# Three x tiles transposed on TensorE, the fourth by DMA transpose, its plain load moved behind

## The chip, the cores and the metric

One core of one Trainium2 chip. The metric is the device time of one execution in microseconds (us), as the median of several executions. The kernel computes a gated mix of a linear-attention block and a token-mixing MLP for one sequence of 2048 tokens and 512 features, in bf16.

## The reference, cut to what matters

```python
x = A_x                                     # [1, 2048, 512]
g = _sigmoid((x * gate_w).sum(-1, keepdims=True))
a = _A_ref(x, A_wqkv, A_wo)                 # q, k, v = x @ wqkv; 32 heads of 16; linear attention; @ wo
b = _B_ref(x, B_w1, B_b1, B_w2, B_b2)       # layernorm; tokens mixed by w1, gelu, w2
return g * a + (1 - g) * b
```

The change touches only the opening of the kernel: the first step is `k = x @ wk` for 16 tiles of 128 tokens. A matmul on TensorE contracts over the partitions, so it needs x transposed (features on partitions). The kernel gets some of the transposed tiles by transposing on TensorE (PE) and the others by a DMA transpose straight from DRAM.

## The kernel before

The parts that matter. PE is TensorE, DVE is VectorE, ACT is ScalarE and SP is SyncE; the results of the matmuls stand in PSUM until DVE or ACT copies them out. The PSUM tiles are named in the profiles: `kacc` for the k matmuls, `gacc` for the products of x with phi(k) (phi is the positive map that the linear attention applies to k), `uacc` for the first matmuls of the token-mixing MLP. `xs` holds x with tokens on partitions, `xT` holds it transposed, `wk_sb` is the k part of the weight in four chunks of 128 rows. The first x tiles and the wk chunks are loaded on two queues (SP is `nc.sync`, ACT is `nc.scalar`):

```python
    load_x(nc.sync, 0, 1)
    load_x(nc.scalar, 1, 1)
    load_wk(nc.sync, 0)
    load_x(nc.scalar, 2, 1)
    load_x(nc.sync, 3, 1)
    for k, q in ((1, nc.scalar), (2, nc.sync), (3, nc.scalar)):
        load_wk(q, k)
    load_xT(4, 2)                 # DMA transpose of tiles 4 and 5
    load_xT(6, 2)
    load_x(nc.sync, 4, 4)
    for t0, n in ((8, 4), (12, 4)):
        load_xT(t0, n)
        load_x(nc.sync, t0, n)
    # ... wq, w1, wv, wo follow on the same queue
```

PE starts with six warm-up matmuls on constants. Then four x tiles are transposed on PE and copied out of PSUM (`transpose_tile`), and the k matmuls of the first tiles run chunk by chunk, as the chunks arrive:

```python
    HEADS = 4
    transpose_tile(0, False)      # False: copied out by DVE, True: by ACT
    transpose_tile(1, True)
    transpose_tile(2, False)
    ln_step(0)
    for k in range(2):
        for t in range(HEADS - 1):
            k_part(t, (k,))
    transpose_tile(HEADS - 1, True)
    ln_step(1)
    for t in range(HEADS):
        k_part(t, range(2 if t < HEADS - 1 else 0, ND))
        k_phi(t)
    LAG = 4
    # ...
    for t in range(HEADS, NT):
        k_part(t, range(ND))
        k_phi(t)
        g_tile(t - LAG)           # the gacc matmuls: x tile (t - 4) with phi(k)
        # ... statistics of the layernorm on DVE
```

Of the kernel before, what the change touches and what calls it, by code (L numbers as in the profile page):

```python
# [8 lines left out]
ALU = mybir.AluOpType  # L9
AX = mybir.AxisListType  # L10
# [5 lines left out]
def kernel(  # L16
# [13 lines left out]
    nc = tc.nc  # L30
    P = nc.NUM_PARTITIONS
# [9 lines left out]
    ND = D // P  # L41
# [25 lines left out]
    def keep(shape, dtype, name):  # L67
        return persist.tile(shape, dtype, name=name, tag=name)

    def bank(name, dtype=FP32):  # L70
        return ps.tile([P, SC], dtype, name=name, tag="bank")

    xs = keep([P, NT, D], BF16, "xs")
    hs = keep([P, NT, D], BF16, "hs")
    xT = keep([P, ND, S], BF16, "xT")
# [9 lines left out]
    Z32 = keep([P, ND * 40], BF16, "Z32")  # L85
# [7 lines left out]
    ident = keep([P, P], BF16, "ident")  # L93
    maskH = keep([P, 8], BF16, "maskH")
    maskQ = keep([P, 2], BF16, "maskQ")
    gw_b = keep([P, D], BF16, "gw_b")
    brow = keep([P, P], BF16, "brow")
# [10 lines left out]
    mhalf = keep([P, TPC], FP32, "mhalf")  # L108
    ones_f = keep([P, 1], FP32, "ones_f")
    warm = nc.const_aps.tensor(1.0, (P, SC), BF16)  # L110

    def mm(o, lhsT, rhs, start, stop, **kw):
        nc.tensor.matmul(o, lhsT=lhsT, rhs=rhs, start=start, stop=stop, **kw)  # L113

    def block_mask(m, cols, width):
        nc.gpsimd.memset(m, 1.0)
        nc.gpsimd.affine_select(
            out=m, in_=m, compare_op=ALU.is_ge, fill=0.0, base=0,
            pattern=[[-HEAD, cols], [0, width]], channel_multiplier=1,
        )  # L120
        nc.gpsimd.affine_select(
            out=m, in_=m, compare_op=ALU.is_ge, fill=0.0, base=HEAD - 1,
            pattern=[[HEAD, cols], [0, width]], channel_multiplier=-1,
        )
# [3 lines left out]
    def load_x(q, t0, n):  # L128
        q.dma_start(out=xs[:, t0 : t0 + n, :], in_=x_view[:, t0 : t0 + n, :])

    def load_wk(q, k):
        q.dma_start(out=wk_sb[:, k, :], in_=wqkv_view[:, k, D : 2 * D])

    def load_xT(t0, n):
        nc.sync.dma_start(
            out=xT[:, :, t0 * P : (t0 + n) * P], in_=X[t0 * P : (t0 + n) * P, :], transpose=True
        )
# [2 lines left out]
    load_x(nc.scalar, 1, 1)  # L140
    load_wk(nc.sync, 0)
    load_x(nc.scalar, 2, 1)
    load_x(nc.sync, 3, 1)
    for k, q in ((1, nc.scalar), (2, nc.sync), (3, nc.scalar)):
        load_wk(q, k)
    load_xT(4, 2)
    load_xT(6, 2)
    load_x(nc.sync, 4, 4)
    for t0, n in ((8, 4), (12, 4)):
        load_xT(t0, n)  # L150
# [3 lines left out]
    for c, (j0, nb) in enumerate(w1_chunks):  # L154
        w = wpool.tile([P, NT, FB * P], BF16, name="w1c", tag="wc")
        w1c.append(w)
        for t0 in range(0, NT, 8) if c == 0 else (0,):
            t1 = t0 + 8 if c == 0 else NT
            nc.sync.dma_start(
                out=w[:, t0:t1, : nb * P], in_=w1_view[:, t0:t1, j0 * P : (j0 + nb) * P]  # L160
# [2 lines left out]
            nc.sync.dma_start(out=wv_sb[:], in_=wqkv_view[:, :, 2 * D : 3 * D])  # L163
            nc.sync.dma_start(out=wo_sb[:], in_=wo_view)

    nc.vector.memset(ones_f[:], 1.0)
    nc.vector.memset(mhalf[:], -0.5)
    nc.vector.memset(Z32[:], 0.0)
    nc.gpsimd.memset(ident[:], 0.0)
    nc.gpsimd.affine_select(  # L170
        out=ident[:], in_=ident[:], compare_op=ALU.not_equal, fill=1.0, base=0,
        pattern=[[-1, P]], channel_multiplier=1,
    )
    block_mask(maskH[:].rearrange("p (a b) -> p a b", b=1), 8, 1)

    nc.vector.tensor_reduce(
        out=maskQ[:], in_=maskH[:].rearrange("p (a m) -> p m a", m=2), op=ALU.max, axis=AX.X
    )
    nc.gpsimd.memset(brow[:], 0.0)

    def load_small():
        nc.gpsimd.dma_start(out=brow[0:NF, :], in_=B_b1.rearrange("(f q) -> f q", q=P))
        nc.gpsimd.dma_start(out=brow[NF : NF + NT, :], in_=B_b2.rearrange("(f q) -> f q", q=P))
        nc.gpsimd.dma_start(
            out=gw_b[:], in_=gate_w.rearrange("(o d) -> o d", o=1).to_broadcast([P, D])
        )
# [11 lines left out]
    def transpose_tile(t, on_act):  # L198
        pt = bank("pt", BF16)
        for k in range(ND):  # L200
            nc.tensor.transpose(pt[:, k * P : (k + 1) * P], xs[:, t, k * P : (k + 1) * P], ident[:])  # L201
        dst = xT[:, :, t * P : (t + 1) * P]
        src = pt[:].rearrange("p (k s) -> p k s", k=ND)
        if on_act:
            nc.scalar.activation(out=dst, in_=src, func=ACT.Copy)  # L205
        else:
            nc.vector.tensor_copy(out=dst, in_=src)
# [13 lines left out]
    def k_part(t, ks):  # L221
        if t not in kaccs:
            kaccs[t] = bank("kacc")
        for k in ks:
            mm(
                kaccs[t][:], xT[:, k, t * P : (t + 1) * P], wk_sb[:, k, :],
                k == 0, k == ND - 1,
            )

    def k_phi(t):  # L230
        phi(pk[:, t, :], kaccs.pop(t))
# [11 lines left out]
    def ln_shift(g):  # L243
        s = slice(g * TPC, (g + 1) * TPC)
        nc.vector.scalar_tensor_tensor(  # L245
            out=nmr[:, s], in0=mv[:, s, 0], scalar=-1.0, in1=rstd[:, s],
            op0=ALU.mult, op1=ALU.mult,
        )

    def ln_apply(t):  # L250
        nc.scalar.activation(  # L251
            out=hs[:, t, :], in_=xs[:, t, :], func=ACT.Identity,
            scale=rstd[:, t : t + 1], bias=nmr[:, t : t + 1],
        )
# [3 lines left out]
    def g_tile(t):  # L258
        if not gacc:
            gacc.extend(bank("gacc") for _ in range(ND))  # L260
        for k in range(ND):
            mm(gacc[k][:], xs[:, t, k * P : (k + 1) * P], pk[:, t, :], t == 0, t == NT - 1)
# [15 lines left out]
    def ln_step(u):  # L278
        ln_stats(u)
        if u % TPC == TPC - 1:  # L280
            ln_rstd(u // TPC)

    HEADS = 4
    transpose_tile(0, False)
    transpose_tile(1, True)
    transpose_tile(2, False)
    ln_step(0)
    for k in range(2):
        for t in range(HEADS - 1):
            k_part(t, (k,))  # L290
    transpose_tile(HEADS - 1, True)
    ln_step(1)
    for t in range(HEADS):
        k_part(t, range(2 if t < HEADS - 1 else 0, ND))
        k_phi(t)
    LAG = 4
    LN_LAG = 3
    APPLY = 9
    for t in range(HEADS, NT):
        k_part(t, range(ND))  # L300
        k_phi(t)
        g_tile(t - LAG)
        if t > LAG:
            ln_step(t - LN_LAG)
        if t == TPC - 1 + LN_LAG:
            load_small()
        if t >= APPLY:
            ln_apply(t - APPLY)
        if t % TPC == 0 and t >= 2 * TPC:
            ln_shift(t // TPC - 2)  # L310
# [143 lines left out]
    for j in range(NB0, NF):  # L454
        c, jj = divmod(j, FB)
# [18 lines left out]
        out=gg[:], in0=gth[:], scalar1=0.5, scalar2=0.5, op0=ALU.mult, op1=ALU.add  # L474
    )
    nc.vector.tensor_scalar(
        out=c1[:], in0=gth[:], scalar1=-0.5, scalar2=0.5, op0=ALU.mult, op1=ALU.add
# [3 lines left out]
    for t in range(NT):  # L481
        c, tl = divmod(t, TPC)
        aps = bank("aps")
        for j in range(ND):
# [3 lines left out]
            out=a_sc[:], in_=aps[:], func=ACT.Identity,  # L488
            scale=gg[:, t : t + 1], bias=c2[:, t : t + 1],
        )  # L490
        for c0, W in ((0, D - P), (D - P, P)) if t == NT - 1 else ((0, D),):
            cs = slice(c0, c0 + W)
            yps = bank("yps")
            for f in range(NF):
# [6 lines left out]
                out=ot[:, :W], in0=yps[:, :W], scalar=c1[:, t : t + 1], in1=a_sc[:, cs],  # L501
# [35 lines left out]
```

## Time and profile before

| | before |
|---|---|
| device time, median of 3 (lowest to highest) | 164.56 us (164.44 to 164.77) |
| span of the profiled execution | 162.5 us |
| PE busy | 158.1 us (97%) |
| DVE busy / ACT busy | 89.5 / 63.3 us |

The profile page of the kernel before, the lines for the whole span and for the chain that ended last:

```profile
span 162.5 us, 2183 instructions
...
PE 158.1 (97%) x823; PEld 72.8 (45%) x837; DVE 89.5 (55%) x210; ACT 63.3 (39%) x97; POOL 17.5 (11%) x34
...
## 4 chain that ended last, share of the span: by engine, by line
PE 97%; issue 0%; DVE 0%
```

The chain is PE from end to end. So work that leaves PE's stream is a gain, and work that moves between the other engines is not, unless PE comes to wait for it.

The timeline of PE in the opening of the kernel before (start, duration, engine, line, operation, output<-inputs, shapes, count):

```profile
2.93 0.63 PE L113 MATMUL wps<-const-bfloat16-1.0 128*128 128x512 bf16 x1
3.55 1.47 PE L201 MATMUL pt<-ident,xs 128*128 128x128 bf16 x12
4.82 1.97 PE L113 MATMUL kacc<-wk_sb,xT 128*128 128x512 bf16 x6
6.62 0.39 PE L201 MATMUL pt<-ident,xs 128*128 128x128 bf16 x4
6.84 3.19 PE L113 MATMUL kacc<-wk_sb,xT 128*128 128x512 bf16 x14
9.86 0.59 PE L113 MATMUL gacc<-pk,xs 128*128 128x512 bf16 x2
```

The reader should see the order: twelve transposes of tiles 0 to 2, six k matmuls (wk chunks 0 and 1 of three tiles), then four transposes of tile 3 between 6.62 and 6.84, then fourteen k matmuls, and the first gacc matmul at 9.86. The durations of neighbouring lines overlap because matmuls are pipelined; the useful number is the distance of two starts. The first matmul on chunk 1 waited about 0.1 us (its start at 5.97 is 0.34 us after the one before it).

The timeline of SP's DMA queue in the kernel before, without the first line and those after 3.70 (the duration is the time to issue, not to land):

```profile
1.27 0.41 SPq L132 DMA_DIRECT2D wk_sb<-in_A_wqkv_dram  x1
1.73 0.42 SPq L129 DMA_DIRECT2D xs<-in_A_x_dram  x1
2.20 0.43 SPq L132 DMA_DIRECT2D wk_sb<-in_A_wqkv_dram  x1
3.70 2.74 SPq L135 DMA_TRANSPOSE xT<-in_A_x_dram  x2
```

The DMA view of the kernel before, restricted to the moment 1.74 us (wk chunk 1, on ACT's queue) and to 3.70 us (the first DMA transpose); the last column is the time from issue to landing:

```profile
wk_sb<-in_A_wqkv_dram ACTq DMA_DIRECT2D x1, 128.0 KB, 4.2
...
xT<-in_A_x_dram SPq DMA_TRANSPOSE x1, 4.0
```

So chunk 1 landed at about 5.9 (5.93 in the trace) and its first matmul started at 5.97; the first DMA transpose (tiles 4 and 5) landed at 7.66, and was wanted at 8.78.

### The profile page before, as it was taken

To read this page: it belongs to the slowest core of one execution; us is meant where nothing else is said; L and a number is where in the kernel's file an instruction comes from. 1 tells how busy PE (TensorE), PEld (TensorE's weight loads), DVE (VectorE), ACT (ScalarE), POOL (GpSimd) and SP (SyncE) were. 2 spreads that over 40 slices of the span, in tenths; PEclk is the share of its full clock that TensorE was granted. 3 is DMA by queue.
4 is the path that set the end of the run, shared out by engine and by line. 5 is a ranking of instruction groups with operands and counts; after the bars stand their busy time and mean duration, and the time that the engine had idled before them with its cause. 6 is when DMAs were issued, how large, how long until landed. Compare 5 with 4: busy or idle time off the path is not lost.

```text
span 162.5 us, 2183 instructions
## 1 busy us (share of the span) xinstructions
PE 158.1 (97%) x823; PEld 72.8 (45%) x837; DVE 89.5 (55%) x210; ACT 63.3 (39%) x97; POOL 17.5 (11%) x34
## 2 busy tenths in 40 slices
PE   7999999999999999999999999999999999999993
PEld 3544444444444444444444444444444444444452
DVE  0599999967999999519995301166211111111112
ACT  3463386648667483212865113111122222111110
POOL 3000711200110000001415500050000000000000
PEclk9999999999999999999999999999999999999999
DMA  5999999999900006600892699822000001110001
GB/s 152 239 212 237 280 316 334 379 386 387 338 12 0 0 0 221 230 4 0 280 318 80 197 325 297 315 99 102 32 32 32 32 32 41 48 44 33 32 32 32
DMA packets 30057, 25.05 MB, mean 154 GB/s; under 512 B 7968, under 2 KB 29472, under 8 KB 30048
## 3 DMA queue, kind: packets, MB, share of 16 engines
q1 hardware_dynamic: 27744, 21.76, 43.4%
q0 software_dynamic: 1440, 2.38, 5.8%
q10 hardware_dynamic: 864, 0.79, 1.4%
q8 instruction: 6, 0.10, 0.3%
q14 instruction: 3, 0.02, 0.0%
HBM read 21.11 MB, written 2.23 MB: 144 GB/s over the span
## 4 chain that ended last, share of the span: by engine, by line
PE 97%; issue 0%; DVE 0%
PE uacc L113 30%; PE yps L113 30%; PE kacc L113 9%; PE aps L113 8%; PE gacc L113 8%; PE qacc L113 8%; PE wps L113 2%; PE pt L201 1%; PE denps L113 1%; PE kvps L113 0%; PE w2ps L113 0%; DVE ot L500 0%; PE pt L330 0%
## 5 line engine op out<-in xcount | busy, mean ns | idle before, releaser
L113 PE MATMUL uacc<-hs,w1c 128*128 128x512 bf16 x219 | 51.0, 379 | 0.4
L113 PE MATMUL yps<-uT,w2c 128*128 128x512 bf16 (+2 forms) x234 | 50.6, 366 | 0.2
L500 DVE SCALAR_TENSOR_TENSOR ot<-yps,c,a_sc 128x512 bf16<-128x512 f32 (+2 forms) x17 | 12.2, 720 | 45.2 <-PE yps L113 42.0
L113 PEld LDWEIGHTS <-w2c 128*128 128x128 bf16 x238 | 22.8, 98 | 25.9
L113 PEld LDWEIGHTS <-w1c 128*128 128x128 bf16 x224 | 21.8, 98 | 26.3 <-issue 0.2
L487 ACT ACTIVATE a_sc<-aps,c,gg 128x512 f32<-128x512 f32 x16 | 12.4, 777 | 46.7 <-PE aps L113 39.6
L324 ACT ACTIVATE uT<-uacc,bcol 128x512 bf16<-128x512 f32 x14 | 9.3, 688 | 21.7 <-PE uacc L113 21.7
L113 PE MATMUL aps<-W2sb,pqT 128*128 128x512 bf16 x63 | 16.2, 379 | 0.1
L113 PE MATMUL kacc<-wk_sb,xT 128*128 128x512 bf16 x63 | 16.2, 385 | 0.0
L113 PE MATMUL qacc<-xT,wq_sb 128*128 128x512 bf16 x63 | 16.2, 379 | 0.0
L113 PE MATMUL gacc<-pk,xs 128*128 128x512 bf16 x62 | 15.5, 379 | 0.1
L251 ACT ACTIVATE hs<-xs,nmr,rstd 128x512 bf16<-128x512 bf16 x16 | 12.8, 805 | 1.9 <-DVE nmr L245 1.9
L211 ACT ACTIVATE e<-qacc 128x512 bf16<-128x512 f32 x16 | 9.6, 597 | 9.2 <-PE qacc L113 8.3
L211 ACT ACTIVATE e<-kacc 128x512 bf16<-128x512 f32 x16 | 9.3, 595 | 6.9 <-PE kacc L113 5.6
L439 POOL DMA_DIRECT2D rex<-rd_dram x16 | 9.5, 602 | 22.9 <-DVE pqT L441 20.5
L215 DVE SCALAR_TENSOR_TENSOR pk<-kacc,e 128x512 bf16<-128x512 f32 x16 | 11.1, 692 | 0.6
L215 DVE SCALAR_TENSOR_TENSOR pqT<-qacc,e 128x512 bf16<-128x512 f32 x16 | 11.1, 692 | 0.6
L235 DVE BATCH_NORM_STATS2 stats<-xs 128x6 f32<-128x512 bf16 x16 | 10.9, 682 | 0.0
L212 DVE TENSOR_SCALAR e<-e 128x512 bf16<-128x512 bf16 x32 | 9.0, 281 | 3.3 <-ACT e L211 3.3
L426 DVE CUSTOM_DVE_ANT_0 junk<-xs,gw_b 128x512 bf16<-128x512 bf16 x16 | 9.8, 683 | 0.0
L276 DVE TENSOR_TENSOR zacc<-zacc,pk 128x512 f32<-128x512 f32 x14 | 9.6, 685 | 0.2
L113 PEld LDWEIGHTS <-xT 128*128 128x128 bf16 x64 | 6.3, 99 | 7.5 <-ACT xT L205 0.4
(61 smaller groups left out, 71.6 us busy)
## 6 DMA issues: line engine op xcount, KB each, us to landing
w2c<-in_B_w_dram SPq DMA_DIRECT2D x8, 896.0 KB, 6.2
w1c<-in_B_w_dram SPq DMA_DIRECT2D x2, 2048.0 KB, 14.0
w1c<-in_B_w_dram SPq DMA_DIRECT2D x3, 1024.0 KB, 11.6
rex<-rd_dram POOLq DMA_DIRECT2D x16, 128.0 KB, 3.5
out_dram<-ot SPq DMA_DIRECT2D x13, 128.0 KB, 1.7
xs<-in_A_x_dram SPq DMA_DIRECT2D x3, 512.0 KB, 5.2
wq_sb<-in_A_wqkv_dram SPq DMA_DIRECT2D x1, 512.0 KB, 6.1
wv_sb<-in_A_wqkv_dram SPq DMA_DIRECT2D x1, 512.0 KB, 10.6
```

Source lines behind the costliest of these rows:

```text
L113: nc.tensor.matmul(o, lhsT=lhsT, rhs=rhs, start=start, stop=stop, **kw)
L211: nc.scalar.activation(out=e[:], in_=acc[:], func=ACT.Exp)
L212: nc.vector.tensor_scalar(out=e[:], in0=e[:], scalar1=1.0, scalar2=PHI_EPS, op0=ALU.min, op1=ALU.add)
L215: nc.vector.scalar_tensor_tensor(out=dst, in0=acc[:], scalar=0.0, in1=e[:], op0=ALU.max, op1=ALU.add)
L235: nc.vector.bn_stats(out=stats[:], in_=xs[:, t, :])
L251: nc.scalar.activation(out=hs[:, t, :], in_=xs[:, t, :], func=ACT.Identity, scale=rstd[:, t : t + 1], bias=nmr[:, t : t + 1],)
L276: nc.vector.tensor_tensor(out=zacc[:], in0=first, in1=pk[:, t, :], op=ALU.add)
L324: nc.scalar.activation(out=uT[:, j, :], in_=acc[:], func=ACT.Gelu_apprx_tanh, bias=bcol[:, j : j + 1])
L426: nc.vector.tensor_tensor_reduce(out=junk[:], in0=xs[:, t, :], in1=gw_b[:], scale=1.0, scalar=0.0, op0=ALU.mult, op1=ALU.add, accum_out=gp ...
L439: nc.gpsimd.dma_start(out=rex[:], in_=src.unsqueeze(1).to_broadcast([8, HEAD, SC]))
L487: nc.scalar.activation(out=a_sc[:], in_=aps[:], func=ACT.Identity, scale=gg[:, t : t + 1], bias=c2[:, t : t + 1],)
L500: nc.vector.scalar_tensor_tensor(out=ot[:, :W], in0=yps[:, :W], scalar=c1[:, t : t + 1], in1=a_sc[:, cs], op0=ALU.mult, op1=ALU.add,)
```

## The change

Intent: PE no longer transposes tile 3. It comes by DMA transpose together with tile 4. The plain load of tile 3 (needed later, for the gacc matmul and the layernorm) moves behind the DMA transposes. A DVE copy that reads x tile 0 and writes into the destination of the first DMA transpose makes that transpose wait until tile 0 has landed (the copied values are overwritten). The memsets on DVE and GpSimd move up only so that this copy comes after them.

```diff
     load_x(nc.scalar, 2, 1)
-    load_x(nc.sync, 3, 1)
     for k, q in ((1, nc.scalar), (2, nc.sync), (3, nc.scalar)):
         load_wk(q, k)
-    load_xT(4, 2)
-    load_xT(6, 2)
+    # ... the memsets and masks, moved up unchanged
+    nc.vector.tensor_copy(
+        out=xT[:, :, 3 * P : 3 * P + 2],
+        in_=xs[:, 0, 0 : 2 * ND].rearrange("p (k c) -> p k c", k=ND),
+    )
+    load_xT(3, 2)
+    load_xT(5, 3)
+    load_x(nc.sync, 3, 1)
     load_x(nc.sync, 4, 4)
 # ... cut
-    HEADS = 4
+    HEADS = 3
 # ... cut
     for k in range(2):
-        for t in range(HEADS - 1):
+        for t in range(HEADS):
             k_part(t, (k,))
-    transpose_tile(HEADS - 1, True)
     ln_step(1)
     for t in range(HEADS):
-        k_part(t, range(2 if t < HEADS - 1 else 0, ND))
+        k_part(t, range(2, ND))
         k_phi(t)
 # ... cut
-        g_tile(t - LAG)
+        if t >= LAG:
+            g_tile(t - LAG)
```

More of the change, by code (lines that the diff above doesn't have):

```diff
@@ L142 @@
     load_x(nc.scalar, 2, 1)
-    load_x(nc.sync, 3, 1)
     for k, q in ((1, nc.scalar), (2, nc.sync), (3, nc.scalar)):
         load_wk(q, k)
-    load_xT(4, 2)
-    load_xT(6, 2)
+    nc.vector.memset(ones_f[:], 1.0)
+    nc.vector.memset(mhalf[:], -0.5)
+    nc.vector.memset(Z32[:], 0.0)
+    nc.gpsimd.memset(ident[:], 0.0)
+    nc.gpsimd.affine_select(
+        out=ident[:], in_=ident[:], compare_op=ALU.not_equal, fill=1.0, base=0,
+        pattern=[[-1, P]], channel_multiplier=1,
+    )
+    block_mask(maskH[:].rearrange("p (a b) -> p a b", b=1), 8, 1)
+    nc.vector.tensor_reduce(
+        out=maskQ[:], in_=maskH[:].rearrange("p (a m) -> p m a", m=2), op=ALU.max, axis=AX.X
+    )
+    nc.gpsimd.memset(brow[:], 0.0)
+    nc.vector.tensor_copy(
+        out=xT[:, :, 3 * P : 3 * P + 2],
+        in_=xs[:, 0, 0 : 2 * ND].rearrange("p (k c) -> p k c", k=ND),
+    )
+    load_xT(3, 2)
+    load_xT(5, 3)
+    load_x(nc.sync, 3, 1)
     load_x(nc.sync, 4, 4)
@@ L164 @@
             nc.sync.dma_start(out=wo_sb[:], in_=wo_view)
-    nc.vector.memset(ones_f[:], 1.0)
-    nc.vector.memset(mhalf[:], -0.5)
-    nc.vector.memset(Z32[:], 0.0)
-    nc.gpsimd.memset(ident[:], 0.0)
-    nc.gpsimd.affine_select(
-        out=ident[:], in_=ident[:], compare_op=ALU.not_equal, fill=1.0, base=0,
-        pattern=[[-1, P]], channel_multiplier=1,
-    )
-    block_mask(maskH[:].rearrange("p (a b) -> p a b", b=1), 8, 1)
-    nc.vector.tensor_reduce(
-        out=maskQ[:], in_=maskH[:].rearrange("p (a m) -> p m a", m=2), op=ALU.max, axis=AX.X
-    )
-    nc.gpsimd.memset(brow[:], 0.0)
     def load_small():
```

## The prediction

> **What bounds the kernel now.** TensorE. The page shows PE busy for 158.1 of 162.5 us at the full granted clock; the chain of waits is 97% PE. From 6.8 us on, matmuls follow each other at a 0.216 us pitch to the end. What leaves that chain is saved; moved DVE, ACT or DMA work saves nothing.
>
> **The opening (timeline, DMA landings).** x tiles 0, 1, 2 land at 3.50, 3.68, 4.37; wk chunk 0 at 4.16; x tile 3 at 5.71; wk chunks 1, 2, 3 at 5.93, 6.45, 6.62. PE waits for tile 0 (until 3.55), for the copies of tiles 1 and 2 out of PSUM (5.27, 5.54), and for wk chunk 1 (5.97). Then four transposes of tile 3 (6.62 to 6.84), six matmuls, tile 3's four from 8.14, tile 4's from 9.00. The first DMA transpose (tiles 4, 5) issues at 3.70, after x tile 1 landed (its semaphore slot makes it wait), and lands at 7.66; the second (6, 7) at 8.80.
>
> **What the change does.**
> 1. Removes four PE transposes of 0.055 us from the chain: -0.22 us. Certain.
> 2. Removes one ACT copy (0.60 us): off the chain.
> 3. Takes x tile 3 (128 KB) out of the early loads. wk chunk 2 moves into its place and should land near 5.7. Chunk 1, on which PE waits, is third on the ACT queue and competes with the third SP load as before: about 5.9 again, gain 0, perhaps 0.1 to 0.2.
> 4. The hold is a DVE copy of 128x8 (about 0.1 us, from the small DVE operations) after x tile 0. The transpose then issues near 3.7, as before: the old slot wait did the same by accident.
> 5. Tiles 3 and 4 by DMA transpose: same start, no x tile 3 ahead, landing 7.2 to 7.7. PE now wants it at 7.70 (6.62 + six matmuls, less the weight load). This is the tight spot: 0 to 0.5 us of margin, where before it had 1.1. A stall would eat the 0.22.
> 6. Tiles 5 to 7: landing about 9.4 (8.80 plus half of the 1.14 between the old two), wanted at 10.3. Later SP loads slip by about 1 us: x tile 3 by 12 (wanted 14.8), tiles 8 to 11 at 14.3 to 14.7 (was 13.52; wanted 15.5), w1 near 27.6 (wanted 33). No wait.
> 7. DVE is nearly full from 8 to 32 us; pk of the last tile is done at 31.85, its matmul runs at 32.31. DVE starts from the first exp, which also comes 0.22 sooner, so this margin stays.
>
> The Trainium skill ("DMA: Bandwidth & Descriptors", "Issuing engines are not separate DMA queues") says that transfers of different issuers share the same 16 DMA engines and interleave; in the trace wk chunks 1 to 3, from two issuers, land within 0.7 us. So taking out a load need not bring the awaited one sooner.
>
> **Prediction.** 164.56 - 0.22, a little less for wk, a little more for a possible stall: 164.35 us, 8 in 10 between 164.0 and 164.8. Faster by over 2%: 0.005; within 2%: 0.985; slower: 0.01.
>
> **What would show it.** 12 transposes on PE instead of 16; first gacc matmul near 9.65 (was 9.86), first uacc near 32.95 (was 33.17); no PE wait for the transposed tile; PE gap-free after 7 us.
>
> **What would make it wrong.** Tiles 3 and 4 landing after 7.7 (each 0.1 late costs 0.1), or their packets slowing wk chunks 1 and 3; chunk 1 landing much sooner (more gain); tiles 8 to 11 later than 15.5.

## The result, and the profile after

| | before | after |
|---|---|---|
| device time, median of 6 (lowest to highest) | 164.50 us (164.10 to 164.77) | 164.14 us (164.02 to 164.64) |
| ratio, 95% interval | | 0.9984 (0.9966 to 1.0002) |
| span of the profiled execution | 162.5 us | 162.5 us |
| PE busy | 158.1 us | 157.5 us |

A ratio here and below is the mean time of one kernel's fast runs over that of the other's fast runs of the same rounds, so it is not quite the ratio of the medians.

The time is inside the predicted range, 0.21 us below the predicted 164.35. The range also holds the time of the kernel before, so the time alone would not tell a right mechanism from a wrong one. But the two profiles have equal spans. The profiled executions took 164.22 (before, a quick one for that kernel) and 164.19 us (after, an ordinary one). A single pair of profiles therefore doesn't show where the gain is; it has to be taken apart.

The page of the kernel after, the lines that answer to those shown of before:

```profile
span 162.5 us, 2175 instructions
...
PE 157.5 (97%) x819; PEld 72.5 (45%) x833; DVE 89.4 (55%) x211; ACT 62.8 (39%) x96; POOL 17.5 (11%) x34
...
## 4 chain that ended last, share of the span: by engine, by line
PE 94%; DMA 3%; issue 1%; ACTq 1%; DVE 0%
```

The timeline of PE in the opening of the kernel after:

```profile
2.93 0.63 PE L113 MATMUL wps<-const-bfloat16-1.0 128*128 128x512 bf16 x1
3.47 1.32 PE L206 MATMUL pt<-ident,xs 128*128 128x128 bf16 x12
4.62 0.38 PE L113 MATMUL kacc<-wk_sb,xT 128*128 128x512 bf16 x1
5.19 0.61 PE L113 MATMUL kacc<-wk_sb,xT 128*128 128x512 bf16 x2 [0.19 <-ACT xT L210]
6.16 3.83 PE L113 MATMUL kacc<-wk_sb,xT 128*128 128x512 bf16 x17 [0.36 <-DMA wk_sb<-in_A_wqkv_dram]
9.82 0.59 PE L113 MATMUL gacc<-pk,xs 128*128 128x512 bf16 x2
```

The four transposes at 6.62 are gone, and seventeen k matmuls run without a break from chunk 1 to the first gacc matmul. In front of them is now a visible wait for wk chunk 1. "DMA 3%" in the page's chain is the flight of that load (4.4 us), at the end of which the wait ends. It is not new: before, chunk 1 was also the last thing PE waited for, but the wait was short enough to hide under the modelled end of the matmul ahead of it.

The timeline of SP's DMA queue in the kernel after, without the first line and those after 7.05:

```profile
1.27 0.89 SPq L132 DMA_DIRECT2D wk_sb<-in_A_wqkv_dram  x2
3.64 3.36 SPq L135 DMA_TRANSPOSE xT<-in_A_x_dram  x2
7.05 1.06 SPq L129 DMA_DIRECT2D xs<-in_A_x_dram  x2
```

The DMA view of the kernel after, restricted to 1.74 us (wk chunk 1, on ACT's queue) and to 3.64 us (the first DMA transpose):

```profile
wk_sb<-in_A_wqkv_dram ACTq DMA_DIRECT2D x1, 128.0 KB, 4.4
...
xT<-in_A_x_dram SPq DMA_TRANSPOSE x1, 4.1
```

The first DMA transpose issues where it did before (3.64 against 3.70) and lands at 7.72. Its first weight load on PE started at 7.88, so the margin was 0.16 us. Chunk 1 landed at 6.12, which is 0.19 us later than in the profile of before, and this ate the 0.22 us that the transposes had cost. The open question was whether that lateness belongs to the change or to the execution.

### The profile page after: what moved, and what is told of

Its sections match the earlier page's. It is cut to its first block, busy times and chain, and to the rows that moved or that the text cites. A ratio compares the mean times of both kernels' runs of the same rounds, so it can differ in the third digit from the quotient of the medians.

```text
span 162.5 us, 2175 instructions
## 1 busy us (share of the span) xinstructions
PE 157.5 (97%) x819; PEld 72.5 (45%) x833; DVE 89.4 (55%) x211; ACT 62.8 (39%) x96; POOL 17.5 (11%) x34
## 4 chain that ended last, share of the span: by engine, by line
PE 94%; DMA 3%; issue 1%; ACTq 1%; DVE 0%
PE uacc L113 30%; PE yps L113 30%; PE aps L113 8%; PE qacc L113 8%; PE gacc L113 8%; PE kacc L113 8%; DMA wk_sb<-in_A_wqkv_dram 3%; PE denps L113 1%; ACTq L129 1%; PE kvps L113 0%; PE w2ps L113 0%; DVE ot L505 0%; PE pt L335 0%
```

## The experiments

Two theories stood at the start. **A**: the gain is the four transposes, 0.22 us; the landing of chunk 1 is scatter of single executions. **B**: the change itself makes chunk 1 later and mostly eats its own gain. A third, **C**, was added after the first four runs. Each run below has its edit relative to the changed kernel, unless said otherwise.

To compare traces, the opening was cut at two PE instructions: the start of the first matmul on wk chunk 1, and the start of the first gacc matmul. All numbers are starts in the traces, in us. "Clock" is the moment from which the trace's clock record shows the full TensorE clock; it is missing in two traces (there the spacing of the transposes falls from 0.107 us to 0.06 between 4.1 and 4.5).

| kernel | first matmul on chunk 1 | from there to the first gacc | from there to PE's end | chunk 1 landed | clock full from | time of that execution |
|---|---|---|---|---|---|---|
| before | 5.97 | 3.889 | 149.83 | 5.93 | 5.58 | 164.22 |
| before, again | 5.91 | 3.892 | 149.83 | 5.42 | 5.66 | 164.16 |
| after | 6.16 | 3.666 | 149.83 | 6.12 | none | 164.19 |
| after, again | 6.03 | 3.666 | 149.83 | 5.99 | none | 164.07 |
| after, third | 6.04 | 3.666 | 149.83 | 6.00 | 3.50 | 164.07 |
| no hold | 5.99 | 3.666 | 149.83 | 5.95 | 3.86 | 164.03 |
| 4 dummy transposes | 5.81 | 3.892 | 149.83 | 5.48 | 4.82 | 164.05 |
| 16 dummy transposes | 5.97 | 4.563 | 149.83 | 5.25 | 5.84 | 164.90 |

The third column is the change: 3.89 with four transposes, 3.67 without. The fourth column is constant: nothing after the first gacc matmul differs. What varies between executions of one kernel is the second column. The third can be compared because the full clock came before that stage began in all eight. Chunk 1's landing did not always set the second: before, again and with 16 dummy transposes it had landed 0.5 and 0.7 us before its first matmul, and the clock was full only from 5.66 and 5.84.

### Before, again (`e1_before_again`): the kernel before against itself

> The kernel before, unchanged, against itself: how far two equal kernels differ, and a second profile of its opening. Ratio 1.000, interval about +-0.0015. Theory A (the gain is the four transposes, 0.22 us, and the landing of wk chunk 1 is noise of single executions): chunk 1 lands anywhere from 5.8 to 6.2. Theory B (with x tile 3 out of the way the DMA transpose reaches the engines sooner and delays wk chunk 1, which eats most of the 0.22): chunk 1 again at 5.93 +-0.05.

Measured: 164.44 us median, ratio 0.9998 (0.9981 to 1.0016). So two equal kernels agree, with an interval of 0.18% on either side. Chunk 1 landed at 5.42, half a microsecond sooner than in the first profile of the same kernel. The scatter that theory A needs exists, and is wider than the 5.8 to 6.2 that A gave it; theory B's 5.93 +-0.05 fell.

### After, again (`e2_after_again`, and `e12_after_third` on another chip)

> The changed kernel, unchanged: a second profile and a tighter ratio. Theory A: ratio 0.9987 (0.22 of 164.4), chunk 1 of wk landing anywhere from 5.8 to 6.2. Theory B: chunk 1 again at 6.12 +-0.05, first uacc matmul again within 0.1 of the kernel before's, ratio 0.9995 to 1.000.

> The changed kernel on the chip of the next two, for comparison, and a third profile. Theory A: ratio 0.9987 within its interval; 3.67 us from the matmul on wk chunk 1 to the first gacc matmul and 149.83 us from there to PE's end, as in the other profiles; only the moment at which chunk 1's matmul starts varies (5.8 to 6.2 so far), with the landing of chunk 1 and with the moment at which the tensor clock is released.

Measured: 164.06 us, ratio 0.9981 (0.9962 to 0.9999), and 164.09 us, ratio 0.9981 (0.9968 to 0.9995). Both intervals exclude 1, the first of them only just. Both profiles have the 3.666 us, and the first uacc matmul starts at 33.00 and 33.02 (before: 33.17 and, again, 33.11). Theory B's 0.9995 lies inside the first interval and on the edge of the second; it falls only by the three ratios of the changed kernel together, 0.9982 +-0.0009 (an estimate, weighted by their intervals). Chunk 1 landed at 5.99 and 6.00, so in this version it is often near 6.0; that PE would have started sooner with the 5.42 of the run above can't be read from these traces alone.

The three ratios are gains of 0.26 to 0.31 us (of 164.4), a little more than the 0.22 us of the transposes. The intervals contain 0.22, and what the rest would be was not settled.

### No hold (`e3_no_hold`)

```diff
-    nc.vector.tensor_copy(
-        out=xT[:, :, 3 * P : 3 * P + 2],
-        in_=xs[:, 0, 0 : 2 * ND].rearrange("p (k c) -> p k c", k=ND),
-    )
```

> The changed kernel without the copy that holds the first DMA transpose. It should then issue near 2.2 instead of 3.64. If its packets compete with the early loads: x tile 2 later than 4.34 or wk chunks 1 to 3 later by 0.3 to 1 us, time 0.3 to 0.8 us more than the changed kernel. If the hold is idle: the same time within 0.1, and tiles 3 and 4 landing near 6.5. Nothing that PE does changes.

Measured: 164.17 us, ratio 0.9985 (0.9968 to 1.0003), against 0.9981 with the hold on the same chip: the same. The transpose issued at 2.20 as expected, but took 1.65 us to issue and landed at 7.27, not near 6.5; with the hold it landed at 7.25, 7.58 and 7.72 in three profiles. Tile 2 (4.39) and chunk 1 (5.95) landed where they do with the hold. So the hold costs and gains nothing that these intervals show, and an earlier issue buys little: issued 1.44 us sooner than in the first profile, the transpose has its first packet at 4.40 instead of 5.08. That it stands behind the wk loads in its queue is the likely reason, not a shown one.

### Four dummy transposes (`e4_dummy4`)

```diff
             k_part(t, (k,))
+    spare = bank("spare", BF16)
+    for k in range(ND):
+        nc.tensor.transpose(spare[:, k * P : (k + 1) * P], xs[:, 2, k * P : (k + 1) * P], ident[:])
     ln_step(1)
```

> The changed kernel with four PE transposes (of tile 2, into a bank that nobody reads) put back where the transposes of tile 3 stood: undoes the PE part alone. Theory A: 0.22 us more than the changed kernel, ratio to before 1.000. Theory B: the transposes cost 0.22 after the wait for chunk 1, so 0.22 more than the changed kernel as well, but chunk 1 late on top: ratio to before 1.0010 or more. If the transposes did not matter at all: the time of the changed kernel.

Measured: 164.09 us, ratio 0.9986 (0.9967 to 1.0004). By the time alone the dummies seem to cost nothing, and theory C was formed: that the gain comes from x tile 3 leaving the early loads. The interval contains 1.000 too, so the time doesn't decide. The trace does: from chunk 1's matmul to the first gacc it took 3.892 us, exactly what the kernel before needs. This execution was quick because chunk 1 landed at 5.48 and its matmul started at 5.81. The chain of waits of this kernel (start, duration, what) shows the dummies standing in it:

```profile
5.37 1.25 PE kacc L113 x5
6.62 0.22 PE spare L298 x4
6.85 3.02 PE kacc L113 x14
9.87 0.86 PE gacc L113 x4
```

### Sixteen dummy transposes (`e6_dummy16`)

The same with `range(4 * ND)`, so that the effect stands clear of the scatter.

> The changed kernel with sixteen dummy PE transposes instead of four. Theory A: 16 x 0.054 = 0.86 us over the changed kernel, 0.65 over the kernel before (ratio 1.004), and 4.53 us from the matmul on chunk 1 to the first gacc matmul. Theory C, or any in which PE has slack there: under half of that.

Measured: 164.86 us, ratio 1.0038 (1.0027 to 1.0050); the expected 1.004 is inside. The stage took 4.563 us, which is 0.897 over the changed kernel, or 0.056 us for each of the sixteen. The chain of waits of this kernel:

```profile
4.99 1.79 PE kacc L113 x6
6.78 0.89 PE spare L299 x16
7.67 3.02 PE kacc L113 x14
10.69 0.86 PE gacc L113 x4
```

PE has no slack at this place: a transpose there costs its full time. Theory A holds for the size of the transposes, and theory C's half of it, that they cost little, fell.

### x tile 3 loaded early (`e5_x3_early`)

This run, the one above and the next two were made on one chip, on which the changed kernel itself was not run.

```diff
     load_x(nc.scalar, 2, 1)
+    load_x(nc.sync, 3, 1)
 # ... cut
-    load_x(nc.sync, 3, 1)
     load_x(nc.sync, 4, 4)
```

> The changed kernel with x tile 3's plain load back in its early place: undoes the load part alone, 12 transposes stay. Theory A (four PE transposes, 0.22 us): from the matmul on wk chunk 1 to the first gacc matmul 3.67 us as in the changed kernel, unless the first DMA transpose lands after about 7.7 and adds a wait up to 0.3; ratio to before 0.9985 to 1.000. Theory C (new: the transposes cost little, as the dummy ones seemed to, and the gain comes from x tile 3 leaving the early loads): ratio 1.000.

Measured: 164.45 us, ratio 1.0012 (0.9997 to 1.0027). There is no gain over the kernel before, although the stage after chunk 1 took the short 3.669 us; the interval only touches the top of what A allowed (0.9985 to 1.000). For the changed kernel on this chip there is only an estimate: the mean of the run above less its sixteen transposes, 164.85 - 0.90 = 163.95 us, against a mean of 164.41 here. By it, theory C was right in its other half: the part of the change that moves the plain load behind is needed, and undoing it costs at least as much as the transposes gave. How it works is not shown. The profiled execution was the slowest of six (164.72). In it wk chunk 0 landed at 5.25 and tile 2 at 5.46 (4.13 and 4.34 after), the page's chain runs through the load of an x tile ("DMA xs<-in_A_x_dram 3%"), and the first matmul on chunk 1 started only at 6.65. But the eight early loads are those of the kernel before, in the same order, and there the two landed at 4.16 to 4.22 and at 4.37 to 4.42; so this lateness does not come from the order alone. The first DMA transpose landed at 8.33, and PE did not wait for it (tile 3's first matmul at 8.59, 0.216 us after the one before). It would make PE wait wherever the rest of the opening is not as late as here, but no trace of such an execution was taken. This stays open between the two: a later transpose, or later early loads.

### Chunks 1 and 2 exchanged between the queues (`e7_swap_wk1`)

```diff
-    for k, q in ((1, nc.scalar), (2, nc.sync), (3, nc.scalar)):
+    for k, q in ((1, nc.sync), (2, nc.scalar), (3, nc.scalar)):
```

> The changed kernel with wk chunks 1 and 2 exchanged between the queues: chunk 1 third on SP, chunk 2 third on ACT. In three of three profiles of this load order the third SP load landed 0.17 to 0.23 us before the third ACT load. If chunk 1 is what PE waits for: its matmul up to 0.2 sooner, then limited by the first DMA transpose landing at about 7.7 (margin 0.16 in the changed kernel's profile), so 0.1 to 0.2 us less time. If not: the same within 0.1.

Measured: 164.19 us, ratio 0.9998 (0.9983 to 1.0013): no gain over the kernel before; against the changed kernel it was not measured. The profile, of the slowest of six executions (164.50), shows another limit. All wk chunks had landed by 5.75, and PE still started chunk 1's three matmuls at 6.16, 6.59 and 6.90: 0.427 us apart at first, twice the usual 0.216. The clock record has the full TensorE clock only from 6.79, and the stage from chunk 1 to the first gacc took 3.98 us.

In eleven of the profiles (all whose records show it, but the last one below) that moment lies anywhere from 3.50 to 6.79. The page "TensorE: Matmul & The Clock Gate" of the Trainium skill (section "Part 1: The HAM clock gate") explains such a pattern: PE starts at half rate and is released by a busy window of about 3.4 us that runs free of the kernel's start. The spread of 3.3 us fits a window of that length. The records fit it better still: in the twelve traces that have one, the last one below included, the full clock lasts 157.013 us (eight) or 160.426 us (four), which are 46 and 47 times their difference of 3.413 us, so its beginning and its end lie on a grid of that step. An estimate from the starts (at the slow clock, 0.427 us for a k or warm-up matmul and 0.107 us for a transpose) has PE busy for 77% or more of the last step before the full clock, and for at most 74% of the step before that one, which did not bring it. So an execution's opening is limited by the landings when the clock comes early, and by PE itself when it comes late; both move the time of a single execution by tenths of a microsecond whatever the change.

### The hold on x tile 2 (`e8_late_hold`)

```diff
-    nc.vector.tensor_copy(
+    nc.gpsimd.tensor_copy(
         out=xT[:, :, 3 * P : 3 * P + 2],
-        in_=xs[:, 0, 0 : 2 * ND].rearrange("p (k c) -> p k c", k=ND),
+        in_=xs[:, 2, 0 : 2 * ND].rearrange("p (k c) -> p k c", k=ND),
     )
```

> The changed kernel with the hold on x tile 2 instead of tile 0, by a GpSimd copy: the first DMA transpose issues near 4.6 and should land near 8.6, about 0.9 later than in the changed kernel. If the margin is as thin as the traces show (tile 3's matmuls want it at 7.7 to 7.9): a PE wait of 0.6 to 0.9 us before tile 3 and 0.6 to 0.9 us more time, ratio to before about 1.003. If PE has slack there: no change.

Measured: 164.99 us, ratio 1.0052 (1.0033 to 1.0072), a larger loss than expected. The first transpose issued at 4.55 and landed at 8.41. The chain of waits of this kernel, around tile 3's first matmul:

```profile
5.03 3.38 PE kacc L113 x12
8.41 0.13 issue
8.54 1.89 PE kacc L113 x8
```

In the profile tile 3's first matmul started 0.505 us after the one before it instead of 0.216, so PE waited 0.29 us. That execution (164.79) had the full clock only from 6.49, so PE reached tile 3 late; that it would have waited longer otherwise is likely, but the others, up to 165.57, have no trace. The margin before the first DMA transpose is as thin as predicted, and its loss costs time.

### One step further: two tiles on PE (`e9_two_tiles`)

```diff
-    load_x(nc.scalar, 2, 1)
 # ... cut
-    nc.vector.tensor_copy(...)          # the hold
+    load_xT(2, 1)
     load_xT(3, 2)
     load_xT(5, 3)
-    load_x(nc.sync, 3, 1)
+    load_x(nc.sync, 2, 2)
 # ... cut
-    HEADS = 3
+    HEADS = 2
 # ... cut
-    transpose_tile(2, False)
```

> One step further: two x tiles transposed on PE, tile 2 by a DMA transpose of its own and tiles 3 and 4 by the next, no hold, plain loads of tiles 2 and 3 behind. Theory A extended: another 0.22 us or more off the chain (four transposes less, 128 KB less before wk), so 0.2 to 0.5 us under the changed kernel, ratio to before 0.996 to 0.997, if tile 2's transpose lands before about 6.6 and tiles 3 and 4 before 7.5. If the DMA transposes are the limit by now (the changed kernel had 0.16 us of margin): a PE wait for xT and the time of the changed kernel or more.

Measured: 163.69 us (163.62 to 163.84), ratio 0.9957 (0.9945 to 0.9969), on the chip where the changed kernel had 0.9981. This beats both kernels, by 0.7 and 0.4 us in the mean, as theory A expected. The timeline of PE in the opening of this kernel:

```profile
3.36 0.74 PE L202 MATMUL pt<-ident,xs 128*128 128x128 bf16 x8
4.39 1.22 PE L113 MATMUL kacc<-wk_sb,xT 128*128 128x512 bf16 x4 [0.29 <-DVE xT L208]
5.86 3.66 PE L113 MATMUL kacc<-wk_sb,xT 128*128 128x512 bf16 x16 [0.25 <-DMA wk_sb<-in_A_wqkv_dram]
9.36 1.03 PE L113 MATMUL gacc<-pk,xs 128*128 128x512 bf16 x4
```

With one load less ahead of them, chunks 0 and 1 are there at 3.94 and 4.17, and PE's last wait of weight is now for chunk 2, until 5.86 (one of about 0.05 us for chunk 3, landed at 6.08, follows). After it come 16 matmuls to the first gacc at 9.36. In the changed kernel's profile on this chip the last wait ended at 6.04 and 17 matmuls followed, to 9.71. The difference of 0.35 us in the opening is 0.18 from the earlier end of the wait and 0.17 from the work behind it, and it is close to the 0.39 us between the mean times. The DMA transposes landed at 6.41 and 7.32, and PE did not wait for them, but the margins are thin (the weight loads for tiles 2 and 3 started at 6.56 and 7.42).

### The same with the hold (`e10_two_tiles_hold`)

The hold of the changed kernel is put back in front of the transposes, with `2 * P` for `3 * P`.

> The same with the hold (the copy after x tile 0): the first DMA transpose issues near 3.7 and lands near 7, so PE should wait for tile 2 by 0.3 to 0.8 us, and the time is 0.2 to 0.6 us more than without the hold: about the changed kernel's. If the hold still costs nothing, the same time within 0.1.

Measured: 164.94 us, ratio 1.0032 (1.0019 to 1.0045): 1.2 us more than without the hold, twice the most that was expected. The hold that cost nothing in the changed kernel is expensive here. The timeline of PE in the opening of this kernel:

```profile
4.60 3.78 PE L113 MATMUL kacc<-wk_sb,xT 128*128 128x512 bf16 x12
9.00 1.90 PE L113 MATMUL kacc<-wk_sb,xT 128*128 128x512 bf16 x8 [0.61 <-DMA xT<-in_A_x_dram]
10.73 0.59 PE L113 MATMUL gacc<-pk,xs 128*128 128x512 bf16 x2
```

The expectation named the wrong transpose. Tile 2's landed at 6.48, nearly as without the hold. The one after it (tiles 3 and 4) can be issued only when the first has been, 1.3 us later; it issued at 5.01 instead of 3.54 and landed at 8.95 instead of 7.32, and PE waited for it until 9.00. Without the hold tile 3 started at 7.63; these 1.37 us are the whole distance between the first gacc matmuls of the two profiles (10.73 and 9.36).

### Only one tile on PE (`e11_one_tile`)

Tiles 1 and 2 each by a DMA transpose of its own, no hold, the plain load of tiles 1 to 3 behind, the statistics of tile 1 moved behind tile 4's k matmuls.

> Where the trade turns: only x tile 0 transposed on PE, tiles 1 and 2 by DMA transposes of their own, no hold, statistics of tile 1 moved behind. Four PE transposes less again (0.22 us), but the first DMA transpose cannot land much before the 6.4 us of the two-tile version, as it stands behind the wk loads in its queue, while PE has done tile 0's four matmuls by about 5.9. If its landing is the limit: tile 1 starts near 6.4, tile 3 near 8.1 instead of 7.42, so 0.5 to 0.8 us more than the two-tile version, ratio to before 0.999 to 1.001. If the DMA transposes keep ahead of PE all the same: 0.2 us less than the two-tile version, ratio 0.994 to 0.995.

Measured: 165.87 us, ratio 1.0074 (1.0052 to 1.0096): clearly worse, and worse than either expectation. The reason expected is not the one in the profile. Tile 1's transpose landed at 6.00, before PE wanted it at 6.49. The timeline of PE in the opening of this kernel:

```profile
4.81 6.34 PE L113 MATMUL kacc<-wk_sb,xT 128*128 128x512 bf16 x20 [0.52 <-DVE xT L208]
10.98 0.38 PE L113 MATMUL gacc<-pk,xs 128*128 128x512 bf16 x1
```

What held PE up last is in the chain of waits of this kernel:

```profile
7.88 5.19 DMA xs<-in_A_x_dram
13.07 0.05 issue
13.12 1.04 PE gacc L113 x4
```

The plain load of tiles 1 to 3 stands behind four DMA transposes in SP's queue. It issued at 7.88 and landed at 13.07, and the gacc matmuls of tile 1 waited for it until 13.12; without the hold and with two tiles on PE they started at 11.09. These 2.03 us are the whole difference between the two profiled executions (165.76 and 163.76). From the first gacc matmul to PE's end it took 150.25 us instead of 149.83.

PE was late before that wait as well: the first nine of the twenty matmuls are about 0.427 us apart, as the full clock comes only at 8.58, later than in any other run here, and the transpose of tiles 3 and 4 landed only at 8.67. But a faster PE would have waited the longer for 13.07, so neither cost time in this execution. That the thinner opening, with PE idle between 4.1 and 4.8, is what made the clock come late is argued from this one profile, not shown; by the estimate above PE was busy for 69% of the step from 1.75 to 5.17, less than in any step that brought the full clock. Five of six executions took 165.76 to 166.13 and one 164.92.

## Why the prediction was right

The prediction was 164.35 us with a range of 164.0 to 164.8; measured were 164.14, 164.06 and 164.09.

1. *Four transposes off the chain, -0.22 us.* Right, and the sharpest result: 3.89 us became 3.666 in each of three profiles, came back to 3.892 with four dummies, and grew to 4.563 with sixteen. The stage behind it is 149.83 us in all of these kernels, so what the opening saves arrives at the end whole.
2. *One ACT copy less is off the chain.* Consistent: nothing on PE waited for it before, and the stage lengths leave no room for a second gain.
3. *Chunk 1 of wk again at about 5.9.* About right in size (6.12, 5.99, 6.00), but the prediction treated as one number what scatters: the same load order put chunk 1 at 5.25 to 6.12, and the kernel before at 5.42 and 5.93. In the first profile this lateness hid the gain; the first gacc came at 9.82 and not near the predicted 9.65, the first uacc at 33.13 and not near 32.95. The other two profiles have 9.69 and 9.71, 33.00 and 33.02. What the prediction took from the Trainium skill, that transfers of different issuers share the same engines, is not contradicted (between 2.5 and 3.0 us of the profile before, SP's queue started packets of 72 KB and ACT's of 70 KB), but no run tests it alone: where the queues were exchanged, the slow clock was the limit.
4. *The hold ends near 3.65 and the transpose issues near 3.7.* Right (3.62 and 3.64; the copy took 0.17 us and not 0.1). Without the hold nothing changed.
5. *The transpose of tiles 3 and 4 is the tight spot.* Right: it landed at 7.72, 7.58 and 7.25, and PE's weight load for it started at 7.88, 7.75 and 7.77, so PE never waited. Held back by another 0.9 us it cost time. That x tile 3 must not stand in front of it was part of this step; with the tile back in front there was no gain (on a chip where the changed kernel was not run), and which wait took it was not seen.
6. *Later loads slip without a wait.* Right: tiles 5 to 7 at 9.24 (9.4 predicted), the plain tile 3 at 10.61 (by 12), tiles 8 to 11 at 13.94 (14.3 to 14.7), w1 at 27.04 (27.6), and no PE wait for any of them.
7. *DVE's margin stays.* Right: pk of the last tile was done at 31.75 (31.85 before), and PE did not wait for it.

What the prediction did not have: the moment at which the tensor clock is released, which lies anywhere from 3.5 to 6.8 us in these profiles, but for the one with 8.58. Single executions of one kernel differ by up to 0.9 us (163.82 to 164.68 for the kernel before on one chip); that this moment and the landings make up that difference is likely, but executions at the two ends have no trace. The gain of 0.2% can be seen in the mean of a few executions only just, but in the length of the right stage it can be seen in one trace.

## What to carry to other kernels

When PE is the chain, cut the trace at two PE instructions on either side of the edit: the length between them shows a gain of 0.2 us exactly, where the times of whole executions scatter by more. Check first that the full clock comes before that stretch: where it came inside it, the stretch took 3.98 us instead of 3.67. Moving work from PE to the DMA engines paid its full time here as long as all that PE wanted had landed in time, the plain loads pushed back behind it too; so follow it step by step, and stop when a step costs more (here two tiles on PE beat three, and one lost). Test every deliberate wait again after such a step: the hold cost nothing that could be measured with three tiles and 1.2 us with two.

## What the Trainium skill lacked or had wrong

- "TensorE: Matmul & The Clock Gate", section "Part 1: The HAM clock gate": it puts the change to the full clock around 4 us into sustained activity, give or take 0.5 us. Here PE's first matmul was at 0.84 us, and the full clock came at 3.50 to 6.79 us in eleven profiles and at 8.58 in one with a thin opening, so 2.7 to 7.7 us into PE's work. The free-running window of about 3.4 us that the same section describes fits all twelve (a grid of 3.413 us); the 0.5 us does not.
- "DMA: Bandwidth & Descriptors" has no issue time of a DMA transpose measured on trn2. Here SP took 1.3 us to issue one of 128 rows and 1.3 us for 256 rows (1.65 when it issued right behind the first loads), 1.5 to 2.7 for 384 and 3.3 to 5.3 for 512, against 0.4 to 0.6 for a plain load of x or wk; the next DMA of the queue waits that long, which is what made the hold cost 1.2 us.
- No page says how much the landing of an early load scatters: the third load on ACT's queue, 128 KB, landed between 5.25 and 6.12 us in equal load orders.
